# Two gate weights fetched in column halves, later, and a gate moved three key tiles down its loop

## The chip, the cores and the metric

The kernel runs on one core of a Trainium2 chip. The metric is the device time of one execution, in microseconds (us); lower is better. The median of six runs of the kernel before the change is 911.34 us (909.53 to 913.8).

## The reference: what is computed

An attention unit without softmax is followed by a maxout layer. Eight batches, 3072 positions each, width 256, key width 64:

```
scores = (z @ z^T) / S ;  attn = max(scores, 0)**2
x      = u * (attn @ v)                       # 8 x 3072 x 256
out    = max(x @ w1, x @ w2) @ w_out          # w1, w2: 256 x 1024, w_out: 1024 x 256
```

Inputs and output are float32 in DRAM; the kernel computes in bf16 with float32 sums.

## The kernel before, in words

**Tiles.** The 3072 positions of a batch are 24 key tiles of 128. Four tiles make a group of 512 queries, so a batch has six groups; two groups make a couple. One block `blk` of the squared scores holds 512 keys by 512 queries. Because the scores are symmetric, a block below the diagonal is the transpose of one above it and is made by a DMA transpose on the SP queue (`mirror`, line 272), not computed again.

**One score pair** (`score_pair`, line 208) makes two key tiles of a block: two matmuls into PSUM (line 222), a Relu of each on ACT (line 235), and one square on DVE (line 243). A group's output is summed by `attn_unit` (line 285, matmuls at line 290) over the 24 key tiles and two column halves `dc` of v.

**The first four groups** of batch 0 are run by a loop written out by hand (lines 616 to 685). `i` is the group, `n` the key tile, and what else happens is hung on pairs `(i, n)`. The order of `n` and `dc` comes from `steps_of` (line 543): the first and the last tiles of a group go one column half after the other, so that one half's sum can be drained while the other still runs. For group 1 the first six and the last six tiles go that way. Each engine's instructions stand in the order in which this code records them, and each engine works through its own list in that order.

**What hangs on group 0 and group 1:**

- `turn_u` (line 196) transposes a group's u (`un`) into `uT` by a DMA on the SP queue. Group 0's is recorded at (0, 14).
- w2 and w1 go into two score blocks that are free at that time. At (0, 18) one column of w2's block is set to zero on DVE (line 661); the load of w2 must wait for that, and the load of w1 stands behind it in the POOL queue (line 663). Each is one DMA of 256 rows. `w15_sb = w1 - w2` is made at (2, 16), and the turn of w2 is recorded at (2, 11), line 674. (max(a, b) = relu(a - b) + b, so only w1 - w2 and w2 @ w_out are needed later.)
- `gate` (line 432) multiplies a group's attention sum by u: one DVE instruction for each column half (line 436). It reads `uT`. Group 0's two halves are recorded in group 1 at n = `first` and `first + 3`, with `first` 11.
- At the end of a group `drain_fast` (line 312) copies the PSUM sums out, on ACT (314) and DVE (315). The next group's matmuls need that PSUM.
- Other loads (`load_u`, `load_z`, `load_v`) go through `load` (line 105) on the POOL queue, mostly behind a small DVE memset that holds them back (lines 191, 145). `load` adds a wait for a matmul only in later couples, where the list `pace` is not empty.

**After these four groups** `second` (line 706) runs the maxout layer of groups 0 and 1, then the loop at line 759 goes on by couples, with the matmuls at line 909. In couple 2, the first of that loop, v of the next batch is loaded in six pieces paced by matmuls.

Of the kernel before, what the change touches and what calls it, by code (L numbers as in the profile page):

```python
# [11 lines left out]
def kernel(  # L12
# [10 lines left out]
    nc = tc.nc  # L23
# [9 lines left out]
    P = 128  # L33
# [3 lines left out]
    GW = G * P  # L37
# [67 lines left out]
    def load(tile_, source):  # L105
        dma = nc.gpsimd.dma_start(out=tile_, in_=source)  # L106
        if pace:
            tc.add_manual_dep(dma.ins, pace[-1].ins.name, AFTER, reason="paced")
# [23 lines left out]
    def zT_pe(lo, n, engine):  # L132
        tp = mm_psum.tile([P, n, P], bf16, name="tpz", tag="mm")
        for j in range(n):
            nc.tensor.transpose(  # L135
                tp[:, j, :], zd_first(lo + j, 1).rearrange("p t h d -> p (t h d)"), ident
            )
        copy = nc.scalar.copy if engine == "act" else nc.vector.tensor_copy
        for k in range(0, n, G):
            copy(zT[:, lo + k : lo + k + G, :], tp[:, k : k + G, :])  # L140
# [55 lines left out]
    def turn_u(b, g):  # L196
        t = upool.tile([P, G, KD, P], bf16, name="uT")
        nc.sync.dma_start_transpose(
            t.rearrange("p a c r -> p (a c) r"), un[b, g].rearrange("p a d -> p (a d)")
        )  # L200
        uT[b, g] = t
# [83 lines left out]
    def attn_unit(b, g, t, acc, dc, first, last):  # L285
        blk, j = divmod(t, G)
        a = A[b, g, blk]
        for half in range(2):
            rows = ds(half * R, R)
            nc.tensor.matmul(  # L290
                a.out(acc[half, dc]),
                v_at(b, t, dc)[rows],
                a.moving(rows, j),
                start=first,
                stop=last,
            )
        if dc == KD - 1 and j == G - 1:
            a.release()
# [4 lines left out]
    def drain(acc, dcs, copy=nc.scalar.copy):  # L303
        hs = {}
        for dc in dcs:
            hs[dc] = new_h()
            copy(hs[dc], acc[1, dc])
        for dc in dcs:
            nc.vector.tensor_add(hs[dc], hs[dc], acc[0, dc])
        return hs  # L310

    def drain_fast(acc, dc):
        hs = [new_h() for half in range(2)]
        nc.scalar.copy(hs[1], acc[1, dc])
        nc.vector.tensor_copy(hs[0], acc[0, dc])
        return hs
# [115 lines left out]
    def gate(b, g, hs):  # L432
        def task(dc):
            if not dc:
                xTs[b, g] = xpool.tile([P, KD, GW], bf16, name="xT")
            nc.vector.scalar_tensor_tensor(  # L436
                out=xTs[b, g][:, dc, :].rearrange("p (t r) -> p t r", r=P),
                in0=hs[dc].rearrange("p (t r) -> p t r", r=P),
                scalar=c2,
                in1=uT[b, g][:, :, dc, :],  # L440
                op0=ALU.mult,
                op1=ALU.mult,
            )

        return [lambda dc=dc: task(dc) for dc in range(KD)]
# [45 lines left out]
    w_out_sb = consts.tile([P, KF, D], bf16)  # L491
# [30 lines left out]
    def emit_pair(wait=0):  # L522
        nonlocal done
        early = done < 12
        finish = score_pair(
            *pairs[done], dve_half=1 if early and done % 3 == 0 else None, halves=done == 0
        )
        done += 1
        if wait:
            due.append((tick + wait, finish))  # L530
        else:
            finish()
# [10 lines left out]
    def steps_of(i):  # L543
        tiles, both = range(NT), range(KD)
        head = edge(i - 1) if i else 0
        tail = NT - edge(i)
        steps = [(n, dc) for dc in both for n in tiles[:head]]
        steps += [(n, dc) for n in tiles[head:tail] for dc in both]
        return steps + [(n, dc) for dc in both for n in tiles[tail:]]

    def pair_slots(i):
        return (
            [1, 3] + list(range(6, 40, 4)),
            list(range(3, 41, 4)),
            list(range(3, 41, 4)),
            list(range(0, 44, 4)),
        )[i]

    def need(b, g, n):
        most = pair_at[b, g, 2 * g]  # L560
        for t in range(n + 1):
            if t // G >= g:
                most = max(most, pair_at[b, g, t // 2] + 1)
        return most

    with tc.manual_schedule():
# [15 lines left out]
        w1_sb, w2_sb = (w.ap.rearrange("p (c f) -> p c f", c=KD) for w in (w1, w2))  # L582
        w2T_sb = w2T.ap.rearrange("p (c k r) -> p c k r", c=KD, r=P)

        def new_acc():
            return {
                (half, dc): acc_tile(2 * half + dc) for half in range(2) for dc in range(KD)
            }
# [27 lines left out]
        for i in range(PLAIN):  # L616
            b, g = groups[i]
            if i:
                acc = new_acc()
            new, slots = {}, pair_slots(i)  # L620
            for slot, (n, dc) in enumerate(steps_of(i)):
                tick += 1
                k = need(b, g, n)
                upto = max(k, min(done + 1, k + AHEAD)) if slot in slots else k
                while done < min(upto, len(pairs)):
                    emit_pair()
                if i == 0 and slot in (10, 22):
                    zT_pe(12 if slot == 10 else 20, 8 if slot == 10 else 4, "act")
                    if slot == 22:
                        for x in z_first:  # L630
                            x.release()
                attn_unit(b, g, n, acc, dc, n == 0, n == NT - 1)
                if n == NT - 1 and i < PLAIN - 1:
                    if i < 2:
                        new[dc] = drain_fast(acc, dc)
                    else:
                        new.update(drain(acc, [dc]))
                if dc:
                    continue
                if i in (1, 2) and n in (5, 8):  # L640
                    k = n // 8
                    nc.vector.tensor_add(sums[k][0], *sums[k])
                    sums[k] = sums[k][0]
                first = 17 if i == 3 else 11
                if i and n == first:
                    gates = gate(*groups[i - 1], sums)
                if i and n in (first, first + 3):
                    gates.pop(0)()
                if i == 0 and n == 14:
                    turn_u(0, 0)  # L650
                if (i, n) in ((1, 8), (2, 1), (2, 19)):
                    load_u(0, i + n // 19, held=True)
                if (i, n) == (3, 14):
                    load_u(0, 4, held=True)
                if (i, n) == (2, 22):
                    turn_u(0, 3)
                if (i, n) in ((1, 16), (2, 14)):
                    turn_u(0, i)
                if (i, n) in ((0, 18), (2, 12)):
                    w_in = ((w2_sb, moe_w2), (w1_sb, moe_w1)) if i == 0 else ((w_out_sb, moe_w_out),)  # L660
                    nc.vector.memset(w_in[0][0][:, 0, 0:1], 0.0)
                    for w_sb, w in w_in:
                        nc.gpsimd.dma_start(
                            out=w_sb, in_=w.rearrange("(c p) f -> p c f", p=P)
                        )
                if later and n % 4 == 0 and (i == 3 or i and n > 12):
                    later.sort(key=lambda block: block[2])
                    mirror(*later.pop(0))
                if i == 2 and n == 16:
                    nc.vector.tensor_sub(w15_sb, w1_sb, w2_sb)  # L670
                    w1.release()
                    w2.release(after=COOL)
                if (i, n) == (2, 11):
                    nc.sync.dma_start_transpose(
                        w2T.ap.rearrange("p (k r) -> p k r", r=P), w2.ap
                    )
                if (i, n) in ((1, 16), (2, 4)):
                    load_z(1, i - 1, held=True)
                if (i, n) in ((2, 17), (2, 20)):
                    turn_z(1, n // 20)  # L680
                if (i, n) == (3, 5):
                    load_z(1, 2, held=True)
                if (i, n) == (3, 17):
                    turn_z(1, 2)
            sums = new
# [73 lines left out]
        for i in range(PLAIN // 2, len(couples)):  # L759
            b, c = couples[i]  # L760
# [3 lines left out]
                b, c, forms, supers=PLAIN_COUPLES.get(i)  # L764
# [62 lines left out]
            f = list(forms.values())  # L827
# [114 lines left out]
        b, c = couples[-1]  # L942
# [31 lines left out]
```

## Time and profile before

| | |
|---|---|
| median of six runs | 911.34 us (909.53 to 913.8) |
| the profiled execution | 912.58 us, of which the span from first to last instruction is 909.8 us |
| TensorE matmul busy | 899.8 us, 99% of the span |
| VectorE busy | 723.0 us, 79% |
| ScalarE busy | 602.1 us, 66% |
| GpSimd busy | 158.8 us, 17% |
| TensorE clock granted, mean | 0.999 |
| DMA packets | 65.4% of 16 engines' span on the SP queue's ring (transposes), 34.6% on the POOL queue's |

PE is TensorE, PEld its weight loads, DVE VectorE, ACT ScalarE, POOL GpSimd, and SP the engine that issues the transposes. A line such as `L290` is line 290 of the kernel before. The chain that ended last is PE for 94% of the span, DMA for 2% and DVE for 1%; the profile follows it back from the last instruction, at each step to what released it.

### The profile page before, as it was taken

What the parts mean: (1) busy time and instruction counts of PE and PEld (TensorE: products, weight loads), DVE (VectorE), ACT (ScalarE), POOL (GpSimd) and SP (SyncE); (2) the same over time, 40 slices, a digit from 0 to 9 for tenths busy, and PEclk for the clock granted to TensorE, in tenths of its full rate; (3) what the DMA queues carried; (4) which work ended last, traced back from release to release, by engine and by line L of the source; (5) the groups of instructions that cost most, each with busy time, mean ns of one, the idle gap of its engine ahead of it and who ended that gap; (6) DMA issues with size and microseconds to landing.
All of it is one profiled execution on the core that took longest, in us unless ns stands there. A gap on an engine that the chain in (4) does not pass through costs nothing.

```text
span 909.8 us, 19350 instructions
## 1 busy us (share of the span) xinstructions
PE 899.8 (99%) x7526; PEld 519.7 (57%) x7526; DVE 723.0 (79%) x1098; ACT 602.1 (66%) x1192; POOL 158.8 (17%) x249
## 2 busy tenths in 40 slices
PE   8999999999999999999999999999999999999998
PEld 4456565565565555665646656566465564655655
DVE  6754688879998799887997979979799788995640
ACT  7887866667666676667676666666766567673445
POOL 4112121211211112201112012021220211201100
PEclk9999999999999999999999999999999999999999
DMA  9999999999899997999979998799999989987202
GB/s 169 178 162 209 191 200 146 174 179 193 135 190 143 169 182 134 202 175 142 178 135 193 169 167 160 134 182 169 152 192 140 188 165 169 163 157 150 73 24 70
DMA packets 410155, 145.59 MB, mean 160 GB/s; under 512 B 361040, under 2 KB 403408, under 8 KB 410064
## 3 DMA queue, kind: packets, MB, share of 16 engines
q1 hardware_dynamic: 359808, 91.79, 65.4%
q0 software_dynamic: 50256, 52.58, 34.6%
q8 instruction: 58, 0.95, 0.5%
q14 instruction: 33, 0.27, 0.1%
HBM read 59.77 MB, written 25.17 MB: 93 GB/s over the span
## 4 chain that ended last, share of the span: by engine, by line
PE 94%; DMA 2%; DVE 1%; SPq 1%; ACT 0%; issue 0%; ACTq 0%; DVEq 0%
PE acc L909 44%; PE d_ps L452 18%; PE o_ps L475 18%; PE s_ps L222 7%; PE o_ps L466 5%; PE acc L290 3%; DMA uT<-un 1%; DMA blk<-blk 1%; SPq L274 1%; DVE blk L243 1%; ACT r_sb L235 0%; PE acc L594 0%; PE w2o_ps L692 0%; DVE xT L436 0%; PE tpz L135 0%
## 5 line engine op out<-in xcount | busy, mean ns | idle before, releaser
L909 PE MATMUL acc<-blk,v_sb 64*128 64x512 bf16 x2208 | 450.7, 376 | 1.0 <-DMA blk<-blk 1.0
L235 ACT ACTIVATE r_sb<-s_ps 128x512 bf16<-128x512 f32 (+3 forms) x672 | 335.9, 559 | 122.3 <-PE s_ps L222 79.0
L909 PE MATMUL acc<-blk,vt 64*128 64x512 bf16 x1512 | 364.1, 376 | 0.0
L909 PEld LDWEIGHTS <-v_sb 64*128 64x128 bf16 x2208 | 177.2, 94 | 135.0 <-issue 7.2
L243 DVE TENSOR_TENSOR blk<-r_sb 128x1024 bf16<-128x1024 bf16 x257 | 172.4, 689 | 85.7 <-ACT r_sb L235 80.4
L459 ACT ACTIVATE g_sb<-d_ps 128x512 bf16<-128x512 f32 x384 | 193.4, 629 | 29.5 <-PE d_ps L452 29.4
L475 PE MATMUL o_ps<-w_out_sb,g_sb 128*128 128x256 bf16 x1536 | 175.5, 273 | 0.0
L909 PEld LDWEIGHTS <-vt 64*128 64x128 bf16 x1512 | 139.2, 94 | 62.5
L452 PE MATMUL d_ps<-xT,w_sb 128*128 128x512 bf16 x768 | 174.0, 379 | 0.0
L475 PEld LDWEIGHTS <-g_sb 128*128 128x128 bf16 x1536 | 150.4, 98 | 17.3
L488 POOL DMA_DIRECT2D out_dram<-o_sb x88 | 64.2, 730 | 487.4 <-ACT o_sb L487 421.5
L487 ACT COPY o_sb<-o_ps 128x512 f32<-128x512 f32 (+1 forms) x98 | 56.3, 577 | 132.9 <-PE o_ps L475 132.9
L786 DVE TENSOR_TENSOR h_sb<-h_sb,acc 128x512 f32<-128x512 f32 x168 | 109.5, 683 | 28.3 <-ACT h_sb L790 20.9
L222 PE MATMUL s_ps<-zT 64*128 64x512 bf16 (+3 forms) x676 | 125.7, 357 | 0.7 <-DVE zT L140 0.7
L452 PEld LDWEIGHTS <-w_sb 128*128 128x128 bf16 x768 | 73.2, 98 | 89.5 <-issue 9.9
L346 DVE TENSOR_TENSOR blk<-blk,blk 128x2048 bf16<-128x2048 bf16 x63 | 77.2, 1225 | 2.2
L350 DVE TENSOR_TENSOR blk<-blk,blk 128x2048 bf16<-128x2048 bf16 x63 | 73.3, 1219 | 6.0 <-DMA blk<-blk 6.0
L342 DVE TENSOR_TENSOR blk<-blk,blk 128x2048 bf16<-128x2048 bf16 x63 | 76.8, 1219 | 0.0
L801 DVE TENSOR_TENSOR blk<-blk,blk 128x2048 bf16<-128x2048 bf16 x63 | 76.7, 1219 | 0.0
L106 POOL DMA_DIRECT2D un<-in_u_dram x94 | 51.0, 556 | 145.2 <-DMA uT<-un 109.5
L436 DVE SCALAR_TENSOR_TENSOR xT<-h_sb,uT 128x512 bf16<-128x512 f32 x96 | 62.0, 685 | 3.8 <-DMA uT<-un 2.5
L241 DVE TENSOR_TENSOR blk<-r_sb 128x512 bf16<-128x512 bf16 (+3 forms) x162 | 46.7, 326 | 19.5 <-ACT r_sb L235 18.4
(49 smaller groups left out, 336.8 us busy)
## 6 DMA issues: line engine op xcount, KB each, us to landing
out_dram<-o_sb POOLq DMA_DIRECT2D x88, 256.0 KB, 4.4
un<-in_u_dram POOLq DMA_DIRECT2D x92, 128.0 KB, 5.2
v_sb<-in_v_dram POOLq DMA_DIRECT2D x18, 512.0 KB, 9.9
blk<-blk SPq DMA_TRANSPOSE x240, 5.1
v_sb<-in_v_dram POOLq DMA_DIRECT2D x11, 256.0 KB, 7.5
zn<-in_z_dram POOLq DMA_DIRECT2D x21, 128.0 KB, 4.3
out_dram<-o_sb SPq DMA_DIRECT2D x6, 256.0 KB, 2.1
blk<-in_moe_w_dram POOLq DMA_DIRECT2D x2, 512.0 KB, 8.1
```

The source lines that it names most:

```text
L222: nc.tensor.matmul(s_ps[h][:, lo[h] :], zT[rows, z_at(b, blk * G + tiles[h]), :], zT[rows, q + lo[h] // P : q + G, :].rearrange("p t c -> ...
L235: nc.scalar.activation(o, s, AF.Relu)
L243: nc.vector.tensor_mul(a[:, k : k + 2, :], r, r)
L342: nc.vector.tensor_add(*alike(f["S1"], f["A21"], f["A22"]))
L346: nc.vector.tensor_sub(*alike(f["S2"], f["S1"], f["A11"]))
L350: nc.vector.tensor_sub(*alike(f["S3"], f["A11"], f["A21"]))
L452: nc.tensor.matmul(d_ps, w15_sb[:, kc, ts(nb, P)], xT[:, kc, :], start=(kc == 0), stop=(kc == KD - 1),)
L459: nc.scalar.activation(g_sb[:, nb, :], d_ps, AF.Relu)
L475: nc.tensor.matmul(o_ps[t // 2][:, t % 2, :], g_sb[:, nb, ts(t, P)], w_out_sb[:, nb, :], start=False, stop=(nb == KF - 1 and t % 2 == 1),)
L786: nc.vector.tensor_add(out, a, b_)
L801: nc.vector.tensor_sub(f["A12"].ap, f["A12"].ap, f["S2"].ap)
L909: mm = nc.tensor.matmul(a.out(acc[name]), w()[rows], a.moving(rows, j), start=name not in opened, stop=left[name] == 0,)
```

## The change

The edit has three parts. The loads of w2 and w1 are recorded at (1, 0) in place of (0, 18), with their memset. Each is cut into two DMAs of 512 columns, so that a row written to SBUF is 1 KB and not 2 KB long, and they go through `load` (with `pace` still empty there). The gates of group 0 are recorded at n = 14 and 17 of group 1 in place of 11 and 14. w_out, 256 wide, keeps its single DMA and its place; the gates of groups 1 and 2 keep theirs (11 and 17).

```diff
-                first = 17 if i == 3 else 11
+                first = (0, 14, 11, 17)[i]
                 if i and n == first:
                     gates = gate(*groups[i - 1], sums)
                 if i and n in (first, first + 3):
                     gates.pop(0)()
...
-                if (i, n) in ((0, 18), (2, 12)):
-                    w_in = ((w2_sb, moe_w2), (w1_sb, moe_w1)) if i == 0 else ((w_out_sb, moe_w_out),)
+                if (i, n) in ((1, 0), (2, 12)):
+                    w_in = ((w2_sb, moe_w2), (w1_sb, moe_w1)) if i == 1 else ((w_out_sb, moe_w_out),)
                     nc.vector.memset(w_in[0][0][:, 0, 0:1], 0.0)
                     for w_sb, w in w_in:
-                        nc.gpsimd.dma_start(
-                            out=w_sb, in_=w.rearrange("(c p) f -> p c f", p=P)
-                        )
+                        w = w.rearrange("(c p) f -> p c f", p=P)
+                        width = min(w.shape[-1], GW)
+                        for f in range(0, w.shape[-1], width):
+                            load(w_sb[:, :, ds(f, width)], w[:, :, ds(f, width)])
```

## The prediction

> **What bounds the kernel now.** I read the page first (busy times, the chain), then the chain of waits over the first 100 us, then the timelines of PE, DVE, POOL and SP around each gap of PE, and last the DMA issues with their time to landing.
>
> ```profile
> PE 899.8 (99%) x7526; PEld 519.7 (57%) x7526; DVE 723.0 (79%) x1098; ACT 602.1 (66%) x1192; POOL 158.8 (17%) x249
> PE 94%; DMA 2%; DVE 1%; SPq 1%; ACT 0%; issue 0%; ACTq 0%; DVEq 0%
> ```
>
> PE is the bound: the end moves only by what is taken out of PE's gaps or added to them. The change moves nothing on PE and touches only the first 50 us, so its stage is where groups 0 to 2 of batch 0 run. The chain of waits there leaves PE for a transfer:
>
> ```profile
> 20.44 10.34 DMA uT<-un
> ...
> 30.88 0.69 DVE xT L436
> 31.57 1.20 DVE blk L243 x2
> ```
>
> The turn of group 0's u is issued at 20.44 and lands at 30.78. The gate on DVE waits for it, and the squares of two score pairs are queued behind the gate. PE's timeline shows what that costs:
>
> ```profile
> 30.42 0.40 PE L290 MATMUL acc<-blk,v_sb 64*128 64x512 bf16 x2
> 32.23 0.82 PE L290 MATMUL acc<-blk,v_sb 64*128 64x512 bf16 x6 [1.41 <-DVE blk L243]
> ...
> 35.15 2.58 PE L290 MATMUL acc<-blk,v_sb 64*128 64x512 bf16 x20 [0.29 <-DVE blk L243]
> ```
>
> Matmul pairs start 0.2155 us apart when nothing is missing (four pairs and a score pair in 1.08 us). From the pair at 30.42 to the first of group 2 at 37.12 there are 19 such steps, 4.09 us, but 6.70 us pass: PE loses 2.61 us here, 1.59 of them at 32.23. Why the turn is slow is in the DMA issues of 20.5 to 21.9 us:
>
> ```profile
> blk<-in_moe_w_dram POOLq DMA_DIRECT2D x2, 512.0 KB, 8.1
> uT<-un SPq DMA_TRANSPOSE x1, 10.3
> ```
>
> w2 and w1 are issued at 20.55 and 21.25, just behind the turn, and land after 6.6 and 9.6 us, w1 at 30.80, in the same moment as the turn. The same turn for group 1, without a large load beside it, lands in 4.5 us. Of the other gaps, 1.02 us at 50.88 are DVE's (a drain behind w1 - w2 and four copies) and one is DMA's:
>
> ```profile
> 82.93 8.91 DMA blk<-blk
> 91.84 0.04 issue
> 91.89 1.04 PE acc L909 x8
> ```
>
> After 91.89 no two matmul starts are over 0.33 us apart: from there to the end PE is full.
>
> **The change, part by part.** *The loads' new place.* In DVE's order the memset now stands behind the two drain copies of group 0, the second of which ends at 22.95 us; POOL then issues. From the DVE memset to the first w packets took about 2 us before (20.24 to 22.4), so they start near 24.9. The turn, issued at 20.44, has the rings to itself from 21.8 (an earlier mirror lands at 21.72) and lands by 25: its own row of group 1 says 24.9. That is 5.9 us earlier, and long before any gate.
>
> *The halves.* POOL issues four DMAs in place of two: 4 x 0.55 to 0.76 us (rows of other loads with as many rows or fewer), 2.2 to 3.0 us against 1.42, done by 26.0; POOL's next work is held until 29.04, so nothing. On the wire the packet records give 172 ns for a 2 KB row of w and 98 ns for a 1 KB row of u: 512 x 172 / 16 = 5.5 us against 1024 x 98 / 16 = 6.3 us, 0.8 us more. The Trainium skill, "DMA: Bandwidth & Descriptors", section "Anatomy of one DMA — SWDGE (gpsimd) path", speaks against halves: a DMA costs about 2.0 us plus its bytes, so two more would bring w 4 us later. The trace's DMAs overlap (w1 was issued 0.7 us behind w2 and landed 3.6 us behind it), so I take 0.8 and keep 4 as the far end. Either way w is in SBUF by 33 to 37 us. Its users are w1 - w2 at 47.59 and the turn of w2, issued at 50.92: over 9 us of cover, and 1 us lost for each one beyond it. The two more DMAs also shift the queue's eight semaphores by two; each load now waits for another one, eight DMAs back, and those landed more than 8 us earlier. No cost.
>
> *The gates.* They move behind one more square each. In steady state DVE starts a square 1.53 us after its scores start on PE (24.81 to 26.34), and PE takes it up 0.74 later. Without the long wait, the square of tiles 18 and 19 ends near 31.3; the first gate (0.60 us from row to row) runs to 31.9, and the square of tiles 20, 21, ready at 31.74, ends at 32.6: PE wanted it at 32.15 and gets it at 32.66, a wait of 0.5. The second gate then holds tiles 22, 23 until 33.85: PE takes them at 33.9, not 33.3, a wait of 0.6. The drain behind adds 0.12. Sum 1.22 us against 2.61: **1.4 us gained.** Much of the 1.22 is there without gates: scores to use takes 2.27 us, and only 1.5 us of matmuls lie between (group 0's end loses 0.55 the same way at 20.28). Ends: gates quite free, 0.9 lost, gain 1.7; gates at full price, 0.77 + 2 x 0.6 + 0.25 = 2.2 lost, gain 0.4. The memset itself (0.06) is nothing.
>
> *What is late next.* All DMA between 25 and 36 us moves later. The mirror issued at 27.06 is needed at slot 4 of group 2: 38.20 before, 36.82 after. And u of group 1, issued at 29.04, now stands behind w; the turn that waits for it moves from 33.79 to 34 to 36, then the mirrors behind it on SP. SP had 1.9 us free before the mirror at 42.18, so that takes up most of it; from 42.18 to 92 SP is never idle.
>
> The second rule is the strictly ordered semaphore: "Queues, rings and completion order" of the same page says that a DMA's completion lands only after every earlier write of its engine, across queues. The rows:
>
> ```profile
> un<-in_u_dram POOLq DMA_DIRECT2D x1, 256.0 KB, 4.7
> blk<-blk SPq DMA_TRANSPOSE x1, 6.6
> ...
> v_sb<-in_v_dram POOLq DMA_DIRECT2D x1, 256.0 KB, 6.5
> blk<-blk SPq DMA_TRANSPOSE x1, 8.9
> ```
>
> The mirror of 27.06 and the u of 29.04 both land at 33.7; the mirror of 82.93 and the v of 85.15 at 91.84 and 91.69. Read as shared bandwidth alone, the mirror PE waits for at 91.89 hangs on SP's full queue, which the change starts no earlier: the 1.4 us would be given back there. Read by the rule, it hangs on the v load, which is paced by PE's own matmuls and so moves forward with them: the gain stays. The mirror's last packets being on the ring by 88 in the trace, I take the rule.
>
> Sum: 909.8 - 1.4 = 908.4 for the span, 911.2 for that execution (912.58). It is 1.2 above the median, and I take the same 1.4 off the median: **909.9 us.** A measurement of this kernel can tell about 0.3%, 2.7 us, from no change; the six runs spread over 4.3 us.
>
> **The rivals.** *A, as above*, 909.9, own range 909.3 to 911.0. *A+:* with the DMA shifted, the wait at 91.89 goes too (another 1.0): 908.9. For it: it is a coincidence of two queues; against: both mostly move together. *B, given back at couple 2:* the SP queue's chain stays where it was and PE only waits longer at 91.89: 911.3, by up to 0.7 more if the 0.8 us of smaller rows come on top. For it: SP without a pause for 50 us. *C, slower:* the mirror of 27.06 now lies wholly beside w, u and z loads. A mirror beside such a row of loads (issued at 45.23, beside w_out and u) took 12.7 us to land; at that price this one lands at 39.8, PE waits from 36.8 for 3.0 us, and 1.4 gained less 3.0 lost gives 912.9; where the two mirrors behind it (used at 51.96 and 53.04, landed 7.1 and 4.5 before) come late too, 914 to 916. It decides from a landing later than 38.2. Against it: w is over by about 33, the 12.7 us hold w_out's 1000 short rows and two u loads, and my own count of its packets gives 35.5 to 37. *That the change doesn't do what it says:* SP reaches the turn at 20.44 in either order, and the memset comes 2.5 us after that, so the loads do stand behind it; I give this nothing of its own.
>
> **How the numbers follow.** A 0.47, A+ 0.13, B 0.22, C 0.18. Faster by over 0.3% (below 908.6): half of A+ and about a fifth of A, where the stall of a usual run is larger than the profiled one: 0.17. Slower by over 0.3% (above 914.1): half of C, with its follow-on waits, and a fifth of B by the spread of the runs: 0.14. Within: 0.69. The range leaves out a tenth on each side, the spread of medians included: 908.2 to 913.2.
>
> **What would show it.** Right: uT lands by 25.5 us, no DVE wait before the first gate, PE's gaps from 30 to 37 near 1.2 us, group 2 starting near 35.7. A: the wait at 91.9 becomes one of about 1 us near 90.5; B: it grows to 2.4; C: a PE wait on `DMA blk<-blk` near 36.8 to 40. Wrong: uT still landing after 28, or a new PE gap after 92 us.

## The result, and the profile after

The change makes the kernel slower: the median is 918.09 us (915.77 to 927.46, 31 runs) against 912.7 us (908.91 to 919.99, 68 runs) for the kernel before, a ratio of 1.0064, 95% interval 1.0047 to 1.0080. Single executions of either kernel spread over some ten us, so medians are compared below, and each profile is read against its own execution. The profiled execution of the changed kernel took 920.61 us, its span is 918.7, its mean granted clock 0.996.

The page after, PE's busy time and the shares of the chain that ended last:

```profile
PE 904.0 (98%) x7526; PEld 519.3 (57%) x7526; DVE 723.0 (79%) x1098; ACT 602.1 (66%) x1192; POOL 160.3 (17%) x251
...
PE 93%; DMA 5%; DVE 2%; ACT 0%; issue 0%; ACTq 0%; DVEq 0%
```

DMA's share of the chain rose from 2% to 5%, and PE is busy 4.2 us longer with the same 7526 matmuls. The chain of waits from 26 us on shows where:

```profile
26.65 0.78 PE acc L290 x7
27.43 15.61 DMA blk<-blk
43.04 0.04 issue
43.08 1.47 PE acc L290 x6
```

The turn of u, which stood in this chain before, is out of it. In its place is the mirror that rival C named: issued at 27.43, needed at slot 4 of group 2, landed at 43.04. PE's timeline around it (start, length, line, operation, in brackets the idle time before and who ended it):

```profile
34.19 2.70 PE L290 MATMUL acc<-blk,v_sb 64*128 64x512 bf16 x22 [0.39 <-DVE blk L243]
...
36.92 0.40 PE L290 MATMUL acc<-blk,v_sb 64*128 64x512 bf16 x2
43.08 1.47 PE L290 MATMUL acc<-blk,v_sb 64*128 64x512 bf16 x6 [5.76 <-DMA blk<-blk]
44.31 0.66 PE L222 MATMUL s_ps<-zT 64*128 64x512 bf16 x2
44.74 1.94 PE L290 MATMUL acc<-blk,v_sb 64*128 64x512 bf16 x8
...
48.37 1.04 PE L290 MATMUL acc<-blk,v_sb 64*128 64x512 bf16 x8
```

PE waits 5.76 us. Then eight matmuls take 1.94 us where they take 1.04 at other times. The stretches of 2 us say why (columns: length, then busy time of PE, PEld, DVE, ACT and POOL, granted clock, DMA share, GB/s):

```profile
40.00:42.00 2.00, 0.00 (x0) 0.00 (x0) 0.00 (x0) 0.00 (x0) 0.00 (x0) 0.72 1.46 110
42.00:44.00 2.00, 0.92 (x6) 0.42 (x7) 0.00 (x0) 0.00 (x0) 0.00 (x0) 0.50 1.22 207
44.00:46.00 2.00, 2.00 (x12) 0.76 (x10) 0.00 (x0) 1.02 (x2) 0.00 (x0) 0.50 1.31 216
46.00:48.00 2.00, 2.00 (x14) 0.87 (x12) 0.69 (x1) 0.95 (x3) 0.00 (x0) 0.57 1.02 215
```

The granted clock falls to 0.50 during the wait and stays there until about 47.7 us. The half-speed matmuls are part of the 4.2 us by which PE is busy longer.

*The account of this execution*, matmul by matmul against the profile before, of which two lines are used:

```profile
37.98 1.04 PE L290 MATMUL acc<-blk,v_sb 64*128 64x512 bf16 x8
...
50.88 1.04 PE L290 MATMUL acc<-blk,v_sb 64*128 64x512 bf16 x8 [0.85 <-DVE h_sb L309]
```

This execution runs 0.37 us late from 10 us on, ahead of everything that the change moves. The gain: the matmul that began at 37.98 before begins at 36.92, 1.06 us earlier, so 1.43 us were gained in between. The wait: the third matmul of that line, at 38.20, begins at 43.08, 4.88 later, so the wait took 5.94 from start to start. The slow clock: the first of group 3 moves from 50.88 to 58.03, 7.15 later, another 2.27. The wait of 1.0 at 91.89 before is gone, because PE itself is late: 91.89 became 97.87, 5.98 later. About 2.2 follow between 395 and 400 us, with 1.6 of waits for a DVE drain (L787) up to 404; e4 and e6 below have the same stall at 43 us and no such waits, so I count these with the spread of executions. The rest is 0.8. The last matmul stands 8.95 us later, and 6.8 without the drains; the medians say 5.4.

### The profile page after: what moved, and what is told of

Same layout as the page of the kernel before. It is cut to its first block, busy times and chain, and to the rows that moved or that the text cites. A ratio compares the mean times of both kernels' runs of the same rounds, so it can differ in the third digit from the quotient of the medians.

```text
span 918.7 us, 19355 instructions
## 1 busy us (share of the span) xinstructions
PE 904.0 (98%) x7526; PEld 519.3 (57%) x7526; DVE 723.0 (79%) x1098; ACT 602.1 (66%) x1192; POOL 160.3 (17%) x251
## 4 chain that ended last, share of the span: by engine, by line
PE 93%; DMA 5%; DVE 2%; ACT 0%; issue 0%; ACTq 0%; DVEq 0%
PE acc L910 42%; PE d_ps L452 18%; PE o_ps L475 17%; PE s_ps L222 7%; DMA blk<-blk 5%; PE o_ps L466 4%; PE acc L290 3%; DVE blk L243 1%; PE acc L594 0%; ACT r_sb L235 0%; PE tpz L135 0%; PE w2o_ps L693 0%; DVE zd L151 0%; DVE blk L342 0%; DVE blk L346 0%
## 5 line engine op out<-in xcount | busy, mean ns | idle before, releaser
L459 ACT ACTIVATE g_sb<-d_ps 128x512 bf16<-128x512 f32 x384 | 193.4, 629 | 29.7 <-PE d_ps L452 29.5
L787 DVE TENSOR_TENSOR h_sb<-h_sb,acc 128x512 f32<-128x512 f32 x168 | 109.5, 683 | 28.3 <-ACT h_sb L791 20.9
```

Source lines behind the costliest of these rows:

```text
L459: nc.scalar.activation(g_sb[:, nb, :], d_ps, AF.Relu)
L787: nc.vector.tensor_add(out, a, b_)
```

## The experiments

All ratios are to the kernel before, measured beside it. A diff is from the kernel that the text names; the landing times are of the profiled execution.

### Parts of the change, one at a time

**e1_gates_only.** The kernel before, with the later gates alone:

```diff
-                first = 17 if i == 3 else 11
+                first = (0, 14, 11, 17)[i]
```

> Only the gates of group 0 are recorded three key tiles later; the loads stay at (0, 18), whole. Theory 'place' (the loads' later start pushes the mirror issued near 27 us, so PE waits for it in group 2): no wait for a mirror near 37 us, since uT lands near 31 and the first gate comes near 31.3: PE's gaps from 30 to 37 us fall from 2.6 to about 1.3, time 1 to 1.5 us below before (ratio 0.9985). Theory 'gates' (the later gates hold DVE at the wrong place and the mirror or group 2 is late for that): slower by about 5 us.

Measured: 915.27 us (909.92 to 919.43), ratio 1.0014 [0.9996, 1.0033]. In the profiled execution PE is 1.39 us ahead of before in group 2 (36.60 against 37.98). It is lost in couple 2, where PE's timeline shows

```profile
93.72 1.04 PE L909 MATMUL acc<-blk,v_sb 64*128 64x512 bf16 x8 [4.22 <-DMA blk<-blk]
94.58 0.44 PE L222 MATMUL s_ps<-zT 64*128 64x512 bf16 x2
94.80 1.93 PE L909 MATMUL acc<-blk,v_sb 64*128 64x512 bf16 x8
```

the same mirror as before at 91.89, now waited for 4.22 us, and the same half-speed matmuls behind it. This is where rival B had the gain given back, but not B's reason. SP issues this mirror at 80.98 and not at 82.93 as before, so its queue was not late. The mirror and the load of v beside it take longer to land; their DMA issues, first of before, then of e1 (microseconds to landing):

```profile
blk<-blk SPq DMA_TRANSPOSE x1, 8.9
v_sb<-in_v_dram POOLq DMA_DIRECT2D x1, 256.0 KB, 6.5
```

```profile
blk<-blk SPq DMA_TRANSPOSE x1, 12.7
v_sb<-in_v_dram POOLq DMA_DIRECT2D x1, 256.0 KB, 8.7
```

The timeline of SP in this run shows one thing more:

```profile
19.04 1.31 SPq L198 DMA_TRANSPOSE uT<-un  x1
```

Nothing up to this point differs from the kernel before, yet SP reaches the turn at 19.04 instead of 20.44. It lands at 22.18, ahead of the w loads, and no gate waits. So the 1.4 us here are not shown to come from the later gates: e3 below has the old gates and an early turn and gains the same 1.43 us. The stall of 1.59 us that the change was to remove is there in some executions only.

**e2_late_whole.** The changed kernel without the halves:

```diff
-                        width = min(w.shape[-1], GW)
+                        width = w.shape[-1]
```

> As the change, but each weight is one load with 2 KB rows. Theory 'place': the mirror's packets still wait for w, PE waits 4 to 6 us near 37 us and the matmul clock drops after it: 5 to 6 us slower than before (ratio 1.006). Theory 'halves' (the 1 KB rows keep the transpose's packets off the rings): mirror lands before 37 us, no such wait, time as before or 1.4 us below it.

Measured: 916.72 us (914.34 to 919.4), 1.0035 [1.0017, 1.0053]. w is through at 31.98 and not at 34.42, and the mirror lands at 36.28, just in time. The mirrors behind it in SP's queue are late all the same; PE's timeline:

```profile
55.53 1.43 PE L290 MATMUL acc<-blk,v_sb 64*128 64x512 bf16 x8 [3.48 <-DMA blk<-blk]
```

The late place costs something without the halves: here the wait comes at 52 to 55.5 us, for a later mirror, and not at 37.

**e3_early_halves.** The halves alone, at the old place, with the old gates (the diff is from the changed kernel):

```diff
-                first = (0, 14, 11, 17)[i]
+                first = 17 if i == 3 else 11
...
-                if (i, n) in ((1, 0), (2, 12)):
-                    w_in = ((w2_sb, moe_w2), (w1_sb, moe_w1)) if i == 1 else ((w_out_sb, moe_w_out),)
+                if (i, n) in ((0, 18), (2, 12)):
+                    w_in = ((w2_sb, moe_w2), (w1_sb, moe_w1)) if i == 0 else ((w_out_sb, moe_w_out),)
```

> Loads in halves, but at (0, 18) as before, and the gates as before (11 and 14). Theory 'place': within 1 us of before, with uT landing near 31 and the DVE wait before the first gate as before, a little longer. Theory 'halves': the turn of u or the mirror behind it starved, PE gap of 4 us or more, slower by about 5 us.

Measured: 913.23 us (910.58 to 920.25), 1.0001 [0.9976, 1.0026]. The turn lands at 22.74 here too, the mirror of 27.43 at 34.63. Two more DMAs and shorter rows cost nothing here, where w is through at 31.35 and the mirror landed long before its use at 37.1.

**e4_late_halves_old_gates.** The changed kernel with the old gates (the first line of the diff above).

> As the change, but with the gates at 11 and 14 as before. Theory 'place': the same as the change, 5 to 6 us slower, a PE wait for the mirror of 4 us or more near 37 us. Theory 'gates': near before.

Measured: 919.36 us (916.44 to 923.28), 1.0072 [1.0047, 1.0097]. The mirror lands at 42.51 and PE waits 5.6 us. The loss belongs to the loads; the later gates neither make nor cure it.

### What holds the mirror

**e5_u_later.** The changed kernel, with u of group 1 loaded ten key tiles later, so that it is not queued behind w, and its turn later too:

```diff
-                if (i, n) in ((1, 8), (2, 1), (2, 19)):
+                if (i, n) in ((1, 18), (2, 1), (2, 19)):
...
-                if (i, n) in ((1, 16), (2, 14)):
+                if (i, n) in ((1, 22), (2, 14)):
```

> The change, with the load of group 1's u recorded at (1, 18) in place of (1, 8) and its turn at (1, 22) in place of (1, 16). Theory 'u beside the mirror' (the mirror starts only when w is through, and is then stretched to 43 us because the load of u, queued right behind w, runs at the same time): the mirror lands by 37 us, PE waits less than 1 us for it, and 4 us or more of the change's loss come back: 1.000 to 1.003 of before. Theory 'halves alone' (the w halves themselves slow the mirror): it still lands after 40 us, ratio 1.006.

Measured: 914.49 us (913.87 to 924.7), 1.0022 [0.9999, 1.0046]. The mirror lands at 36.48 and PE does not wait for it. But the turn is now late itself; on DVE

```profile
50.78 0.69 DVE L436 SCALAR_TENSOR_TENSOR xT<-h_sb,uT 128x512 bf16<-128x512 f32 x1 [8.03 <-DMA uT<-un]
```

the gate waits for it, the drain behind the gate waits too, and PE stops for 7.0 us, until 52.1. (This execution took 921.45 us, well above the median of its kernel.) Without u behind w the mirror is not late; taking that load away this way only moves the stall.

**e6_u_1kb_rows.** The changed kernel, u of group 1 in two DMAs:

```diff
-        step = 2 if b or g > 1 else G
+        step = 2 if b or g > 0 else G
```

> The change, with group 1's u loaded as two DMAs with 1 KB rows in place of one with 2 KB rows, at the same place. Theory 'long rows of u' (each 256 B packet of the mirror waits behind a 2 KB row): the mirror lands 2 us or more earlier, near 38 to 41 us, and the loss falls to 2 to 4 us. Theory 'any load beside the mirror': the mirror still lands near 43, ratio 1.006.

Measured: 917.3 us (915.0 to 926.4), 1.0045 [1.0020, 1.0069]; the mirror lands at 42.60 and PE waits 5.3 us. Cutting u in two does not help the mirror.

**e9_u_first.** The changed kernel with the same u load ahead of w in POOL's queue, its turn where it was:

```diff
-                if (i, n) in ((1, 8), (2, 1), (2, 19)):
+                if (i, n) == (0, 18):
+                    load_u(0, 1, held=True)
+                if (i, n) in ((2, 1), (2, 19)):
```

> The change, with the load of group 1's u recorded at (0, 18), ahead of w in the POOL queue, in place of (1, 8) behind it; its turn stays at (1, 16). Theory 'u beside the mirror': the mirror of group 1 has the rings to itself once w is through (about 32 us) and lands by 36 us; PE waits less than 0.5 us for it; the change's loss is gone and the gates' gain of 1.4 us stays up to couple 2: 0.997 to 1.001 of before, depending on the wait near 92 us. Theory 'w so late is enough to hold the mirror up': a wait of over 2 us near 37 us is left, ratio 1.003 or more.

Measured: 911.56 us (909.81 to 920.84), 1.0000 [0.9972, 1.0029]. The mirror lands at 37.40, PE waits 0.4 us for it. One load moved ahead of another takes the whole loss of 0.64% away.

**e10_u_first_whole.** e9 with w in whole rows (the diff of e2).

> As e9_u_first, with w in whole 2 KB rows. If the halves are a cost of their own (w through 2.4 us later, as in the run with late whole loads): w lands by 32 and the mirror 1 to 2 us earlier than in e9_u_first, time equal or up to 1 us lower. If they are not: the same.

Measured: 911.22 us (909.65 to 920.84), 0.9984 [0.9954, 1.0013]. The mirror lands at 35.30 and PE does not wait. In couple 2 it does:

```profile
92.32 1.89 PE L912 MATMUL acc<-blk,v_sb 64*128 64x512 bf16 x8 [2.48 <-DMA blk<-blk]
```

**e11_u_first_w_early.** The kernel before, with the later gates and u of group 1 loaded ahead of w, and w left at its old place in whole rows:

```diff
-                first = 17 if i == 3 else 11
+                first = (0, 14, 11, 17)[i]
...
-                if (i, n) in ((1, 8), (2, 1), (2, 19)):
+                if (i, n) == (0, 16):
+                    load_u(0, 1, held=True)
+                if (i, n) in ((2, 1), (2, 19)):
```

> The kernel before with the gates three key tiles later and group 1's u loaded at (0, 16), ahead of w at (0, 18). It should have neither the wait at the first gate nor one for the mirror near 37 us. Theory 'SP queue': u's earlier landing frees the queue by about 1 us and the wait near 92 us falls to 1 to 3 us: 0.997 to 1.000 of before. If the wait near 92 has another cause it stays at 4 us or more: 1.002.

Measured: 910.96 us (908.94 to 915.68), 0.9972 [0.9953, 0.9992]: faster than the kernel before and than the changed one. PE's waits from 20 to 110 us, all that the profile has:

```profile
PE acc L290 <- DVE h_sb L309: 0.8, 1, 0.8
PE acc L290 <- DVE blk L243: 0.4, 1, 0.4
PE acc L290 <- DVE blk L663: 0.4, 1, 0.4
PE acc L290 <- DVE zn L145: 0.3, 1, 0.3
```

No wait for DMA is left, neither near 37 nor near 92.

**e12_w_behind_mirror.** e9 with w fourteen key tiles later still, so that the mirror is ahead of it:

```diff
-                if (i, n) in ((1, 0), (2, 12)):
+                if (i, n) in ((1, 14), (2, 12)):
```

> As e9_u_first, with the w halves recorded at (1, 14) in place of (1, 0), so behind the mirror of group 1 and not ahead of it. Theory 'a mirror starts only when the loads ahead of it are through': the mirror issued near 27 us lands by 31 us and PE never waits for it; the mirrors behind it (used near 50 us) now meet w, land 4 to 8 us later than before, and the last of them makes PE wait near 53 us or near 92 us for 1 to 4 us: 1.000 to 1.004 of before.

Measured: 921.31 us (918.32 to 930.05), 1.0070 [1.0034, 1.0106]. The mirror of 26.68 lands at 32.01. A later one meets w, and u, z and w_out queued behind it; its DMA issue (microseconds to landing) and PE's wait for it:

```profile
blk<-blk SPq DMA_TRANSPOSE x1, 19.1
...
PE acc L290 <- DMA blk<-blk: 7.1, 1, 7.1
```

This mirror was issued at 40.38, and SP was held in its issue until 50.22, past the end of w (44.77) and of the u and z loads behind it (48.87). The collision followed w to the next mirrors.

### Mirrors from SP's full stretch, and the clock

**e7_mirrors_early.** e1, with two of the mirrors that are put off to later moved to (1, 0) and (1, 2), to relieve SP before couple 2:

```diff
-                if later and n % 4 == 0 and (i == 3 or i and n > 12):
+                if later and (n % 4 == 0 and (i == 3 or i and n > 12) or (i, n) in ((1, 0), (1, 2))):
```

> Gates late as in the change, loads of w as before, and two of the mirrors that are put off (of group 0's blocks 3 and 4) recorded at (1, 0) and (1, 2), when the SP queue has nothing else to do. Theory 'SP queue' (what the later gates gain is given back at the mirror that couple 2 waits for, which ends the queue's chain of mirrors): the wait near 92 us, 4.6 us with the gates alone, falls under 1 us, and time falls 2 us or more below before: ratio 0.997. Theory 'the wait near 92 hangs on the v load beside it, not on the queue': the wait stays, ratio near 1.001. Risk for both: the mirror of group 1 now stands behind two others and group 2 waits for it near 37 us.

Measured: 924.29 us (917.58 to 928.86), four runs only, 1.0125 [1.0045, 1.0205]. The mirror of group 2's slot 4 now stands behind the two in SP's queue: issued at 34.55, landed at 40.94, PE waits 4.3 us. It says nothing on couple 2, since the new stall comes first.

**e8_pe_kept_busy.** The changed kernel, with 28 matmuls whose result is not used put in the place of the wait, at (2, 4):

```diff
+                if (i, n, dc) == (2, 4, 0):
+                    busy = mm_psum.tile([P, GW], fp32, name="busy", tag="mm")
+                    for _ in range(28):
+                        nc.tensor.matmul(
+                            busy.rearrange("p (a d) -> p a d", a=2),
+                            ident,
+                            vp[0, 0][:, 0:2, :],
+                            start=True,
+                            stop=True,
+                        )
```

> The change with 28 matmuls of 128x512 that nothing uses put on PE ahead of the first matmul that waits for the late mirror (6.0 us at full clock, as long as the wait). Theory 'clock': PE's long wait costs twice, once as a wait and once since the granted clock is halved for about 4.6 us after it (12 steps at 0.43 us in place of 0.2155, 2.5 us); with PE busy the steps after it stay at 0.2155 and time is 2 to 2.5 us below the change (ratio to before 1.004). Theory 'the slow steps have another cause': steps still at 0.43, time as the change or above it.

Measured: 917.37 us (915.44 to 919.01), 1.0045 [1.0028, 1.0062]. PE's timeline, and the clock in the stretch after:

```profile
36.52 6.22 PE L635 MATMUL busy<-v_sb,ident 128*128 128x512 bf16 x28
42.67 0.82 PE L290 MATMUL acc<-blk,v_sb 64*128 64x512 bf16 x6
...
55.36 0.82 PE L290 MATMUL acc<-blk,v_sb 64*128 64x512 bf16 x6 [0.86 <-DVE h_sb L309]
```

```profile
42.00:44.00 2.00, 2.00 (x18) 0.75 (x18) 0.00 (x0) 0.26 (x1) 0.00 (x0) 1.00 1.26 198
```

The mirror lands at 41.57, and the unused matmuls go on for about a microsecond after it (28 x 0.2155 = 6.03 us from 36.52), which this kernel loses. But the clock stays at 1.00, and from the first matmul with the mirror to the first of group 3 it takes 12.69 us (42.67 to 55.36), as before the change (12.68, 38.20 to 50.88), against 14.95 after it (43.08 to 58.03). The halved clock costs 2.26 us of the changed kernel's execution. The medians (918.09 and 917.37, in different sessions) don't show it as clearly, since the unused matmuls outlast the wait and this execution has a wait of 1.5 us in couple 2 besides.

## Why the prediction was wrong

**What held.** The turn of u lands at 23.26, I had said by 25. No gate waits for it; DVE's timeline has the two gates between squares without an idle bracket:

```profile
31.63 0.68 DVE L436 SCALAR_TENSOR_TENSOR xT<-h_sb,uT 128x512 bf16<-128x512 f32 x1
32.23 0.69 DVE L243 TENSOR_TENSOR blk<-r_sb 128x1024 bf16<-128x1024 bf16 x1
32.84 0.69 DVE L436 SCALAR_TENSOR_TENSOR xT<-h_sb,uT 128x512 bf16<-128x512 f32 x1
```

From 30.79 to the first matmul of group 2 at 36.06 PE's gaps sum to 1.18 us, for my 1.22, and up to slot 4 of group 2 the gain is 1.43 us, for my 1.4. The later gates have no part in it: e4, with the old ones, gains the same 1.43 by the early turn alone.

**The step that failed is the landing of the mirror of 27.06**, in rival C: "my own count of its packets gives 35.5 to 37", and a price of 12.7 us at worst. It took 15.61. The count, whose working the prediction does not show, had let the mirror's packets take turns with w's from their issue on. The DMA profile of the changed kernel from 28 to 31 us, when the mirror has been issued, has only packets of POOL's ring, q0:

```profile
DMA packets 351, 0.34 MB, mean 113 GB/s; under 512 B 21, under 2 KB 351, under 8 KB 351
...
q0 software_dynamic: 351, 0.34, 96.1%
```

and from 33 to 41 us both rings are busy and move little:

```profile
DMA packets 1777, 0.74 MB, mean 93 GB/s; under 512 B 1577, under 2 KB 1648, under 8 KB 1776
...
q1 hardware_dynamic: 1560, 0.40, 75.4%
q0 software_dynamic: 216, 0.33, 48.8%
```

The prediction cited the Trainium skill's page "DMA: Bandwidth & Descriptors"; its section "Queues, rings and completion order" also says that each DMA engine takes turns between the rings that it has work for, packet by packet. Before the change the trace agrees for the turn of u, which was issued ahead of w: from 23 to 28 us there are 499 packets of SP's ring, q1, and 433 of q0. I carried this over to the mirror, which is issued behind w, and there it had no packet in these 3 us. That need not contradict the rule: SP was still busy issuing the mirror, so its packets may not have been on the ring yet; no view shows which. The time that SP needs for this issue, in the changed kernel and in the one before:

```profile
27.43 6.83 SPq L274 DMA_TRANSPOSE blk<-blk  x1
```

```profile
27.06 3.25 SPq L274 DMA_TRANSPOSE blk<-blk  x1
```

SP is through with it at 34.26 and 30.31, and the last piece of w lands at 34.42 and 30.80. Side by side (the last column is the mirror's landing less w's):

| kernel | w in | u of group 1 | last of w lands | SP done with the mirror | mirror lands | behind w by |
|---|---|---|---|---|---|---|
| before | early, whole | behind w | 30.80 | 30.31 | 33.68 | 2.9 |
| e1 | early, whole | behind w | 29.97 | 30.20 | 33.44 | 3.5 |
| e3 | early, halves | behind w | 31.35 | 31.04 | 34.63 | 3.3 |
| e11 | early, whole | ahead | 31.08 | 30.70 | 33.48 | 2.4 |
| e10 | late, whole | ahead | 32.99 | 32.85 | 35.30 | 2.3 |
| e2 | late, whole | behind w | 31.98 | 31.79 | 36.28 | 4.3 |
| e5 | late, halves | much later | 33.41 | 33.25 | 36.48 | 3.1 |
| e9 | late, halves | ahead | 34.33 | 33.81 | 37.40 | 3.1 |
| **after** | late, halves | behind w | 34.42 | 34.26 | 43.04 | 8.6 |
| e4 | late, halves | behind w | 33.91 | 33.87 | 42.51 | 8.6 |
| e6 | late, halves | behind w, two DMAs | 34.42 | 34.29 | 42.60 | 8.2 |
| e8 | late, halves | behind w | 33.63 | 33.50 | 41.57 | 7.9 |

In every row SP gets through its issue when w lands, to within 0.5 us. The mirror's first packets move a little sooner: in the changed kernel at 31.8, beside the last of w's packets, of which the last starts at 33.9. After w's landing the mirror needs about 3 us (2.3 to 4.3), but about 8 (7.9 to 8.6) where u has long been queued behind late halves. The packets show what the four slow rows share: u's first packet comes 0.3 to 0.4 us after w's last one, while in the other eight POOL's ring stands empty, or next to it, for 1.5 us or more, and the mirror uses this time. Before the change, from 29.5 to 31.5 us, the mirror has the rings to itself:

```profile
DMA packets 1217, 0.31 MB, mean 156 GB/s; under 512 B 1217, under 2 KB 1217, under 8 KB 1217
...
q1 hardware_dynamic: 1217, 0.31, 86.7%
```

In the changed kernel from 34 to 36 us it shares them with u, and moves 405 packets in the same time.

So the mis-sized term has two parts. From its first issue to its last landing w takes 10.8 us in halves and 9.1 whole (e2), 11.0 and 9.3 in e9 and e10: the halves cost 1.7 us, where I had said 0.8 with 4 as the far end. And u behind w adds 5.6 us (43.04 against 37.40), where I had counted only that its turn would be later. Neither part alone makes PE wait long at this place (e2, e9); together they do. With a landing at 38.2 as the point that decides, C had the right mechanism, and I gave it 0.18. C was short of the loss all the same, 914 to 916 at worst: it had 12.7 us for the landing and nothing for the clock.

**The step that was missing is the clock.** I took a wait of PE at its length. This one cost 2.26 us more, by e8. The Trainium skill's page "TensorE: Matmul & The Clock Gate", section "What's actually happening", has TensorE at half rate after an idle window of about 3.4 us; the runs agree on the half (0.50), but the wait of 2.48 us in e10 sufficed (clock 0.50 from 92.4 to 95.7 us) and one of 1.9 in e3 did not.

The clock also tells how often PE stood still for long, since each of the profiles with a mean clock of 0.998 or less has such a spell at 0.50 and none of the others has. By this mark all 32 executions of the changed kernel had one, none of 20 in e8, 20 of 46 of the kernel before, measured beside e9 to e12, and 3 of 22 in e11. Executions with 0.999 or more have medians of 910.86 us before and 910.82 in e11. So a long stall, which before came in some executions, came in every one after the change; where it stood before is not known, since the profile of before has none. By these medians e11 is faster because it stalls less often, and not by the 1.4 us.

**A's argument against B failed too.** I let the strictly ordered semaphore carry the gain past 91.89, since the mirror there would move with the paced v load. In e1, with the gain and without the late w, v is issued 1.38 us earlier, as I had it, but takes 2.1 us longer to land, and PE waits for the mirror for 4.22 us in place of 1.0. Nor was the stall of 1.59 us a property of the kernel: in e1 and e3 the turn was past before w came. The gain to be had was smaller than one profile said.

**What stays open.** Why a transpose that was issued behind a load gets nothing for up to 4 us while the load runs, and why both rings together crawl at 93 GB/s once the mirror and u share them, no run here tells. Likewise, e11 has no wait in couple 2, e9 one of 0.6 us, e10 one of 2.48 and e1 one of 4.22. SP's queue does not explain it: SP issues the mirror there at 80.35, 80.87, 82.58 and 80.98, and e1's stands between those of e9 and e10.

## What to carry to other kernels

A load that is moved out of the way of one transfer is moved into the way of the next: list every transpose and every load behind the new place, with its deadline, and take as the landing of a transpose issued behind the big load the end of that load plus its own time, here 2.3 to 4.3 us, and about 8 where the next load follows at once. Put the small load that a transpose will meet ahead of the big one in the queue (e9: one load moved, and the ratio to before goes from 1.0064 to 1.0000). Before removing a stall, see in more than one execution that it is there, and add to a long wait of TensorE the slow clock behind it: here waits of 1.9 us and less had none, those of 2.48 and more had it.

## What the runs showed of the hardware that was not expected

- A DMA transpose on SP's ring had no packet from 28 to 31 us while POOL's load ran, and SP was held in its issue for 6.83 us, to within 0.2 us of the load's landing. In the twelve kernels of the table the two times lie 0 to 0.5 us apart. In e12 a mirror issued at 33.25, before the first packet of w at 34.85, was not held so: SP was through with it at 37.99, 6.8 us ahead of w's last landing.
- Rows of 1 KB beside a waiting transpose moved 113 GB/s (133 in e9), rows of 2 KB 188 in e10. Where the transposes' packets were already running as the load came, the two rings together moved 196 GB/s (before the change, 23 to 28 us).
- The granted clock fell to 0.50 in PE's wait of 5.76 us and came back 4.6 us after work had begun again, at a cost of 2.26 us for the matmuls in between.
